# Prologue of a linear-attention and two-MoE kernel: the three chunks' TensorE work interleaved, five masks moved to ScalarE and GpSimd, products of ones added

## The chip, the cores and the metric

The kernel runs on one core of a Trainium2 chip. The metric is the device time of one execution in microseconds (us), as the median of several runs. The engines are called as in the profile: PE (TensorE, matmul; PEld is its weight load), DVE (VectorE), ACT (ScalarE), POOL (GpSimd) and SP (SyncE, which only issues transfers here).

## What is computed

Gated linear attention over 4 batches, 8 heads, 768 positions and a head size of 48; a dense two-layer network with squared ReLU on the 3072 tokens; then a layer of 8 experts of which each token takes one.

```python
def _attn_ref(q, k, v, f_logit):
    f = 1.0 / (1.0 + np.exp(-f_logit))
    for t in range(S):
        state = f[:, :, t, :, None] * state + np.einsum('bhd,bhe->bhde', k[:, :, t], v[:, :, t])
        y[:, :, t] = np.einsum('bhd,bhde->bhe', q[:, :, t], state)

x = attn_out.transpose(0, 2, 1, 3).reshape(B * S, H * D)    # 3072 x 384
h = np.maximum(x @ w_in, 0.0)                               # w_in 384 x 2048
x = h * h @ w_out                                           # w_out 2048 x 384
# experts: argmax of x @ w_gate, then relu(x @ w1[e]) @ w2[e], times the token's gate
```

## The kernel before, in words

The attention is worked in chunks of 128 tokens, 24 in all, and three chunks make a token group of 384 (`G`); there are 8 groups. A chunk has these steps, each a function of the kernel:

- `load_chunk(c)`: SP asks for f (the gate logits), q and k (one tile, `qk`, of three that take turns) and v.
- `sigmoid(c)` on ACT, then `decays(c)` on DVE: two scans of 112 x 517 with small operations between (lines 216 to 225), then `scale_qk(c)`, which multiplies k and q by the running products (lines 235 to 237).
- `scores(c)` on PE: k is transposed (`pk`, line 257), copied to `kt` by ACT (259), and k times q is made for all heads (`pa`, 264). `masked(c)` on DVE multiplies `pa` by the causal mask (271).
- `outputs(c)` on PE: the state times q (300), `pu` = k times v for the next state (310), the masked scores times v (320). In group 0 a product with `spread` (331) puts two of the heads' rows where the dense layer wants them; in other groups two transfers do that (336). ACT copies the result to `xT` (328 to 333).
- `state(c)` on DVE makes the next state `wst` from `pu` (345 to 348).

The dense layer goes over 16 hidden blocks i per group: `moe_h` makes `ph` (line 395 in group 0, plain float32, each product in two instructions; 405 in the others, split into high and low parts), `moe_act` squares it on ACT to `gg`, and `moe_out` makes `po` (435), two blocks behind `moe_h`. In group 0 the weights come in as 64-bit numbers: `stage_job(n)` asks for job n's stage `stg` (line 185, three stages at most), and `convert_job(n)` turns it into `w_raw` with three DVE operations (167, 170, 173) and asks for stage n + 3. Job 2j is a piece of w_in, job 2j + 1 one of w_out, and each serves the hidden blocks 2j and 2j + 1.

Order: PE, ACT, DVE and POOL take their instructions in the order in which the program writes them, SP's is set by a scheduler. The prologue (lines 567 to 601) does chunks 0, 1 and 2 with jobs 0 to 2. Then the loop over groups runs the dense layer of group g, with the attention of group g + 1 put between its blocks by `attention_group`, at fixed block numbers `b`:

```python
b = (1, 6, 10)[m] if g == 1 else 5 * m
while not (yield) == (b, 1):
    pass
```

At `(b, 1)`, after block b, come the scores and the mask of a chunk, at `(b + 1, 0)` the next chunk's decays, at `(b + 2, 1)` its outputs and state, and at `(b + 3, 0)` the next chunk's scaling. In group 0 each block also converts one job, from job 3 on.

Of the kernel before, what the change touches and what calls it, by code (L numbers as in the profile page):

```python
# [57 lines left out]
def gla_moe_moe_kernel(ctx: ExitStack, tc: tile.TileContext, qk, ft, vt, w_in, w_out, w_gate, w_gateT, w_e, q, k, v, f_logit, out, dbg=None):  # L58
# [11 lines left out]
    spread = const.tile([128, 3, 128], F32, name="spread")  # L70
    nc.gpsimd.memset(spread, 0.0)
    for r in range(3):
        for o in (0, 64):
            nc.gpsimd.tensor_copy(spread[:, r, o + D : o + 64], ident[:, o + r : o + D : 3])
# [12 lines left out]
    step_r = const.tile([PR, FL], BF16, name="step_r")
    nc.gpsimd.memset(step_r, PFLOOR)
    nc.gpsimd.memset(step_r[:, ::SEG], 1.0)
    step_f = const.tile([PR, FL], F32, name="step_f")  # L90
    nc.gpsimd.memset(step_f, PFLOOR)
# [55 lines left out]

    ld_t = {}

    def load_chunk(c):  # L150
        t = qk_t[c % 3]
        f = ld.tile([PR, FL], F32, tag="f", name="f")
        v3 = ld.tile([128, H, 64], F32, tag="v", name="v")
        nc.sync.dma_start(out=f, in_=ft[c])
        for i in ((1, 2), (0, 1)) if c == 0 else ((0, 2),):
            for j in range(2):
                nc.sync.dma_start(out=t[64 * j : 64 * j + D, slice(*i)], in_=qk[c, D * j : D * j + D, slice(*i)])
        nc.sync.dma_start(out=v3, in_=vt[c])
        ld_t[c] = t, f, v3

# [69 lines left out]
    def scale_qk(c):  # L230
        t, pr, _ = ld_t[c]
        tl, _ = prep_t[c]
        pairs = lambda a: a.rearrange("p (a b) -> p a b", a=4)
        qd, kd = t[:, 0], t[:, 1]
        nc.vector.tensor_tensor(out=kd, in0=kd, in1=pairs(tl[:, 1:FL])[:, :, 1:], op=ALU.mult)
        nc.vector.tensor_tensor(out=qd, in0=qd, in1=pairs(pr[:, 0 : FL - 1])[:, :, 1:], op=ALU.mult)
        nc.vector.tensor_tensor(out=pmin[0:PR], in0=pmin[0:PR], in1=tl[:, 1:FL:SEG], op=ALU.min)

    def x_tiles(g):
        xT = (  # L240
            xhp.tile([128, 3, G], F32, tag="xl", name="xT0")
            if g == 0
            else xp.tile([128, 3, G], F32, tag="xT", name="xT")
        )
        x_t[g] = xT, xp.tile([128, G], F32, tag="xT3", name="xT3")
# [1 line left out]

    at_t = {}

    def scores(c):  # L250
        t, _, _ = ld_t[c]
        qd, kd = t[:, 0], t[:, 1]
        kt = None
        if c % CPB != CPB - 1:
            pk = ps_a.tile([128, 4, PR], F32, tag="att", name="pk")
            for p in range(4):
                nc.tensor.transpose(out=pk[:, p, :], in_=kd[:, p, :], identity=ident[0:PR, 0:PR])  # L257
            kt = a1.tile([128, 4, PR], F32, tag="kt", name="kt")
            nc.scalar.activation(out=kt, in_=pk, func=AF.Copy)
        pas = [ps_a.tile([128, 4, 128], F32, tag="att", name="pa") for _ in range(2)]  # L260
# [16 lines left out]
    def outputs(c):
        g, m = divmod(c, GC)
        first = c % CPB == 0
        t, _, v3 = ld_t.pop(c)  # L280
        qd = t[:, 0]
        kt, at = at_t.pop(c)
# [8 lines left out]
        if g == 0:  # L291
            y[2] = ps_o.tile([128, DM], F32, tag=f"po{m}", name="y2")[:, 0:C]
        opens = (0, 2, 3) if g == 0 else (0, 2)
        closes = (3,) if g == 0 else (1, 3)
        if not first:
            for s in range(2):
                for b in range(2):
                    for j in range(2):
                        rows, p = slice(64 * j, 64 * j + D), 2 * s + b
                        nc.tensor.matmul(  # L300
                            y[2 * j + s][64 * b : 64 * b + 64],
                            lhsT=wst[c % 2][rows, p, :],
                            rhs=qd[rows, p, :],
                            start=2 * j + s in opens,
                            stop=False,
                        )
        if pu is not None:
            for p in range(4):
                for j in range(2):
                    nc.tensor.matmul(  # L310
                        pu[64 * j : min(64 * j + 64, PR), p, :],
                        lhsT=kt[:, p, 64 * j : min(64 * j + 64, PR)],
                        rhs=v3[:, p + 4 * j, 0:D],
                        start=True,
                        stop=True,
                    )
        for n in (2, 3, 0, 1):
            for b in range(2):
                j, p = n // 2, 2 * (n % 2) + b
                nc.tensor.matmul(  # L320
                    y[n][64 * b : 64 * b + 64],
                    lhsT=v3[:, p + 4 * j, :],
                    rhs=at[:, j, p, :],
                    start=first and n in opens,
                    stop=n in closes,
                )
# [12 lines left out]
    def state(c, pu):
        if pu is None:  # L340
# [242 lines left out]
    pu = outputs(0)  # L583
# [790 lines left out]
```

## Time and profile before

| what | value |
|---|---|
| median of 3 runs (lowest, highest) | 805.92 us (803.7, 806.31) |
| the profiled execution's own time | 804.5 us |
| span of the profiled execution | 802.8 us |
| PE busy | 775.1 us, 97% |
| DVE busy | 561.3 us, 70% |
| ACT busy | 413.4 us, 51% |
| POOL busy | 76.2 us, 9% |
| chain that ended last, shares by engine | PE 85%, issue 6%, DVE 4%, DMA 2% |

The span runs from the first to the last instruction; the rest of the execution's time lies around it. A line of the timeline gives start and duration in us, engine, line, operation, what it writes and reads, and how many instructions were merged; in brackets the engine's idle time before it and what ended that. Ends of PE's instructions are modelled, and POOL's times are rough.

### The profile page before, as it was taken

What the parts mean: (1) busy time and instruction counts of PE and PEld (TensorE: products, weight loads), DVE (VectorE), ACT (ScalarE), POOL (GpSimd) and SP (SyncE); (2) the same over time, 40 slices, a digit from 0 to 9 for tenths busy, and PEclk for the clock granted to TensorE, in tenths of its full rate; (3) what the DMA queues carried; (4) which work ended last, traced back from release to release, by engine and by line L of the source; (5) the groups of instructions that cost most, each with busy time, mean ns of one, the idle gap of its engine ahead of it and who ended that gap; (6) DMA issues with size and microseconds to landing.
All of it is one profiled execution on the core that took longest, in us unless ns stands there. A gap on an engine that the chain in (4) does not pass through costs nothing.

```text
span 802.8 us, 15135 instructions
## 1 busy us (share of the span) xinstructions
PE 775.1 (97%) x5657; PEld 723.2 (90%) x5657; DVE 561.3 (70%) x1309; ACT 413.4 (51%) x822; POOL 76.2 (9%) x108
## 2 busy tenths in 40 slices
PE   5899999999999999999999999999999999999994
PEld 4566579999999999999999999998999999999994
DVE  7999689768757767857757844668566676666650
ACT  2224376454464454455455454762566666666651
POOL 2000000000000000000000002000432232223110
PEclk9999999999999999999999999999999999999997
DMA  9787511111130121130120015321877777776760
GB/s 274 216 262 231 142 40 41 52 53 51 40 91 26 45 82 46 45 101 27 46 71 1 1 39 199 110 76 52 289 221 224 220 219 228 211 213 208 212 205 18
DMA packets 39410, 98.93 MB, mean 123 GB/s; under 512 B 5502, under 2 KB 9314, under 8 KB 39200
## 3 DMA queue, kind: packets, MB, share of 16 engines
q1 hardware_dynamic: 35744, 88.42, 37.3%
q0 software_dynamic: 3584, 9.46, 3.3%
q8 instruction: 46, 0.75, 0.4%
q14 instruction: 36, 0.29, 0.1%
HBM read 88.16 MB, written 10.24 MB: 123 GB/s over the span
## 4 chain that ended last, share of the span: by engine, by line
PE 85%; issue 6%; DVE 4%; DMA 2%; POOL 1%; ACT 1%; POOLq 0%; SPq 0%; DVEq 0%; ACTq 0%
PE po L435 25%; PE ph L405 23%; PE ph L982 11%; PE qo L1002 11%; PE ph L395 3%; PE pa L264 3%; PE py L320 3%; PE py L300 1%; PE pu L310 1%; DMA xT<-xT 1%; PE px L642 1%; PE pk L257 1%; DMA out<-o,ids 1%; PE pl L485 0%; DVE tl L216 0%
## 5 line engine op out<-in xcount | busy, mean ns | idle before, releaser
L411 ACT ACTIVATE gg<-ph 128x384 f32<-128x384 f32 x128 | 62.8, 491 | 184.6 <-PE ph L405 134.0
L614 DVE TENSOR_TENSOR w_lo<-raw,w_hi 128x768 fp32r<-128x768 f32 x112 | 107.0, 957 | 31.7 <-ACT w_hi L613 31.7
L418 DVE TENSOR_TENSOR gl<-gg,gh 128x384 fp32r<-128x384 f32 x112 | 62.1, 555 | 85.3 <-ACT gh L416 84.0
L405 PE MATMUL ph<-xh,w_lo 128*128 128x384 f32 x336 | 118.7, 353 | 0.9 <-ACT gg L411 0.9
L405 PE MATMUL ph<-xl,w_hi 128*128 128x384 f32 x336 | 114.4, 341 | 0.6 <-DVE xl L163 0.6
L405 PE MATMUL ph<-xh,w_hi 128*128 128x384 f32 x336 | 113.9, 339 | 0.0
L435 PE MATMUL po<-w_hi,gl 128*128 128x384 f32 x336 | 113.4, 338 | 0.0
L435 PE MATMUL po<-w_hi,gh 128*128 128x384 f32 x336 | 113.2, 337 | 0.0
L435 PE MATMUL po<-w_lo,gh 128*128 128x384 f32 x336 | 112.8, 336 | 0.0
L986 ACT ACTIVATE hh<-ph 128x256 fp32r<-128x256 f32 (+1 forms) x120 | 44.3, 370 | 103.3 <-PE ph L982 91.5
L613 ACT ACTIVATE w_hi<-raw 128x768 fp32r<-128x768 f32 x112 | 93.6, 837 | 0.0
L982 PE MATMUL ph<-xh,w_lo 128*128 128x256 f32 x312 | 88.9, 285 | 0.0
L982 PE MATMUL ph<-xl,w_hi 128*128 128x256 f32 x312 | 87.6, 281 | 0.0
L982 PE MATMUL ph<-xh,w_hi 128*128 128x256 f32 x312 | 87.5, 280 | 0.0
L459 DVE SCALAR_TENSOR_TENSOR junk<-rows,wgb 128x384 f32<-128x384 f32 x144 | 79.9, 555 | 3.3
L987 DVE SCALAR_TENSOR_TENSOR hl<-ph,hh 128x256 fp32r<-128x256 f32 (+1 forms) x120 | 48.7, 405 | 42.4 <-ACT hh L986 39.5
L1002 PE MATMUL qo<-w_hi,hl 128*128 128x384 f32 x208 | 70.4, 339 | 0.0
L1002 PE MATMUL qo<-w_hi,hh 128*128 128x384 f32 x208 | 70.4, 338 | 0.0
L1002 PE MATMUL qo<-w_lo,hh 128*128 128x384 f32 x208 | 70.1, 337 | 0.0
L412 ACT ACTIVATE gg<-gg 128x384 f32<-128x384 f32 x128 | 67.3, 526 | 4.1
L405 PEld LDWEIGHTS ph<-xh,w_lo 128*128 128x128 f32 x336 | 63.0, 188 | 6.9 <-issue 3.1
L405 PEld LDWEIGHTS ph<-xl,w_hi 128*128 128x128 f32 x336 | 63.1, 188 | 1.0 <-DVE xl L163 0.8
(235 smaller groups left out, 1498.0 us busy)
## 6 DMA issues: line engine op xcount, KB each, us to landing
raw<-w_e SPq DMA_DIRECT2D x120, 384.0 KB, 3.6
qk<-qk SPq DMA_DIRECT2D x46, 192.0 KB, 3.6
v<-vt SPq DMA_DIRECT2D x24, 256.0 KB, 3.7
stg<-w_in SPq DMA_DIRECT2D x8, 768.0 KB, 6.1
stg<-w_out SPq DMA_DIRECT2D x8, 768.0 KB, 6.0
f<-ft SPq DMA_DIRECT2D x24, 226.2 KB, 3.1
xs<-rows SPq DMA_DIRECT2D x8, 577.5 KB, 3.3
wgb<-w_gateT SPq DMA_DIRECT2D x1, 1536.0 KB, 7.1
```

The lines of the kernel that those rows point to most:

```text
L405: nc.tensor.matmul(ph, lhsT=w[:, sl], rhs=x[:, k, :], start=(n == 0), stop=(n == 8))
L411: nc.scalar.activation(out=gg, in_=ph, func=AF.Relu)
L412: nc.scalar.activation(out=gg, in_=gg, func=AF.Square)
L418: nc.vector.tensor_tensor(out=gl, in0=gg, in1=gh.bitcast(F32), op=ALU.subtract)
L435: nc.tensor.matmul(po[m], lhsT=a[:, sl], rhs=w[:, ws], start=(i == 0 and n == 0), stop=(i == NF - 1 and n == len(terms) - 1),)
L459: nc.vector.scalar_tensor_tensor(out=junk, in0=rows[:, m, 0:DM], scalar=1.0, in1=wgb[0][:, e, :], op0=ALU.mult, op1=ALU.mult, accum_out=lg ...
L613: nc.scalar.activation(out=hi, in_=src, func=AF.Copy)
L614: eng.tensor_tensor(out=lo, in0=src, in1=hi.bitcast(F32), op=ALU.subtract)
L982: nc.tensor.matmul(ph, lhsT=wslice(s, w, (i * 3 + k) * 128, 128), rhs=x[:, k, :], start=(n == 0), stop=(n == 8))
L986: nc.scalar.activation(out=hh, in_=ph, func=AF.Relu)
L987: nc.vector.scalar_tensor_tensor(out=hl, in0=ph, scalar=0.0, in1=hh.bitcast(F32), op0=ALU.max, op1=ALU.subtract)
L1002: nc.tensor.matmul(out_t[s][m], lhsT=x[:, sl], rhs=wslice(s, w, 3 * F2 + i * DM, DM), start=(i == 0 and n == 0), stop=(i == 7 and n == 2),)
```

## The change

Five things, all but the last two in the prologue.

- POOL sets `step_r` and `step_f` first; `spread` is filled after chunk 0's mask.
- The three chunks' steps are cut into smaller functions and interleaved on PE. The chunks' outputs of group 0 go to the three banks that the dense layer's `po` uses, `pu` of chunks 0 and 1 to the banks of `ph`. f of chunk 1 is asked for ahead of v of chunk 0.
- 72 and then 24 products of a tile of ones with itself (bfloat16, 128 x 128) are issued on PE, before chunk 0's transposes and before chunk 1's. Nothing reads them.
- The masks of chunks 0, 1, 3, 4 and 5 are made in two steps: ACT copies the scores to SBUF, and POOL's `affine_select` sets the upper part to 0.
- Jobs 0, 1 and 2 are converted after chunk 2's outputs, and chunk 3's decays, state and scaling leave the prologue: they now come at blocks 0 and 1 of the loop, and chunk 3's scores at block 2 (before: block 1).

```diff
+    step_r = const.tile([PR, FL], BF16, name="step_r")
+    nc.gpsimd.memset(step_r, PFLOOR)
+    nc.gpsimd.memset(step_r[:, ::SEG], 1.0)
...
     def masked(c):
         kt, pas = at_t[c]
         at = a1.tile([128, 2, 4, 128], F32, tag="at", name="at")
         for j in range(2):
-            nc.vector.tensor_tensor(
-                out=at[:, j], in0=pas[j], in1=mask[:, None, :].to_broadcast([128, 4, 128]), op=ALU.mult
-            )
+            if c in (0, 1, 3, 4, 5):
+                nc.scalar.activation(out=at[:, j], in_=pas[j], func=AF.Copy)
+                nc.gpsimd.affine_select(
...
+                )
+            else:
...
+    def first_banks(c):
+        po = [ps_o.tile([128, DM], F32, tag=f"po{m}", name="y") for m in range(GC)]
+        first_y[c] = [po[0][:, 0:C], po[0][:, C : 2 * C], po[2][:, 0:C], po[1][:, 0:C]]
+
+    def first_key_values(c):
+        if c < GC - 1:
+            pu = ps_h.tile([128, G], F32, tag="ph", name="pu")[:, 0 : 4 * D]
+        else:
+            pu = ps_a.tile([128, 4 * D], F32, tag="att", name="pu")
...
+    def first_values(c):
+        y, ts = first_y[c], slice(c * C, (c + 1) * C)
+        scores_values(c, y, (3, 2, 0, 1), () if c else (0, 2, 3), (3,))
+        nc.scalar.activation(out=x_t[0][1][:, ts], in_=y[3], func=AF.Copy)
+
+    def first_rows(c):
+        xT, xT3 = x_t[0]
+        y, ts = first_y[c], slice(c * C, (c + 1) * C)
+        for r in range(3):
+            nc.tensor.matmul(y[r], lhsT=spread[:, r, :], rhs=xT3[:, ts], start=False, stop=r > 0)
+        for r in (2, 0, 1):
+            nc.scalar.activation(out=xT[:, r, ts], in_=y[r], func=AF.Copy)
...
     def attention_group(g):
         for m in range(GC):
             c = g * GC + m
-            b = (1, 6, 10)[m] if g == 1 else 5 * m
+            b = (2, 6, 10)[m] if g == 1 else 5 * m
+            if c == GC:
+                while not (yield) == (0, 1):
+                    pass
+                decays(c)
+                while not (yield) == (1, 1):
+                    pass
+                state(c - 1, first_pu.pop(c - 1))
+                scale_qk(c)
...
+    def fill(n):
+        for _ in range(n):
+            nc.tensor.matmul(idle[:, 0:128], lhsT=ones_bf, rhs=ones_bf, start=True, stop=True)
+
+    fill(72)
     x_tiles(0)
     sigmoid(0)
     sigmoid(1)
     decays(0)
     scale_qk(0)
+    key_rows(0)
     scores(0)
-    sigmoid(2)
     decays(1)
     masked(0)
...
+    first_key_values(0)
+    fill(24)
+    sigmoid(2)
     scale_qk(1)
-    state(0, pu)
+    state(0, first_pu[0])
+    key_rows(1)
+    first_banks(0)
+    first_values(0)
     scores(1)
     decays(2)
     masked(1)
-    pu = outputs(1)
+    first_rows(0)
+    first_key_values(1)
     scale_qk(2)
-    state(1, pu)
+    state(1, first_pu[1])
+    key_rows(2)
+    first_banks(1)
+    state_queries(1, first_y[1], (0, 2, 3))
     scores(2)
+    first_values(1)
+    masked(2)
+    first_rows(1)
+    first_key_values(2)
+    first_banks(2)
+    state_queries(2, first_y[2], (0, 2, 3))
+    first_values(2)
+    first_rows(2)
     load_chunk(3)
     convert_job(0)
-    masked(2)
-    pu = outputs(2)
-    sigmoid(3)
     load_chunk(4)
     convert_job(1)
-    decays(3)
-    state(2, pu)
-    scale_qk(3)
     convert_job(2)
+    sigmoid(3)
```

How the order moves is told at three places. On SP, before, from chunk 3's f on. qk0, qk1, qk2 are the tiles of chunks 3, 4 and 5 here, stg_346 is the stage of job 3, stg_396 that of job 4:

```order
L154 DMA f_336<-ft 112x517
L157 DMA qk0_148<-qk 48x1024 x2
L154 DMA f_386<-ft 112x517
L158 DMA v_337<-vt 128x512
L157 DMA qk1_149<-qk 48x1024 x2
L154 DMA f_443<-ft 112x517
L158 DMA v_387<-vt 128x512
L185 DMA stg_346<-w_out 128x768
L157 DMA qk2_150<-qk 48x1024 x2
L185 DMA stg_396<-w_in 128x3x256
L158 DMA v_444<-vt 128x512
```

The same place of the changed program, where stg_487 is job 3's stage and stg_499 job 4's:

```order
L149 DMA f_477<-ft 112x517
L160 DMA qk0_142<-qk 48x1024 x2
L149 DMA f_489<-ft 112x517
L163 DMA v_479<-vt 128x512
L149 DMA f_566<-ft 112x517
L160 DMA qk1_143<-qk 48x1024 x2
L163 DMA v_491<-vt 128x512
L160 DMA qk2_144<-qk 48x1024 x2
L163 DMA v_568<-vt 128x512
L190 DMA stg_487<-w_out 128x768
L190 DMA stg_499<-w_in 128x3x256
```

The stage of job 3 stood ahead of q, k and v of chunk 5, and now stands behind them.

On DVE, before, from job 1 (the first three rows) to the scaling of chunk 3's k and q; the mask of chunk 2 and job 0 stand ahead of these rows:

```order
L167 TENSOR_SCALAR w_raw<-stg 128x768
L170 SCALAR_TENSOR_TENSOR w_raw<-stg,w_raw 128x768
L173 SCALAR_TENSOR_TENSOR w_raw<-stg,w_raw 128x768
L216 SCALAR_TENSOR_TENSOR tl<-f,step_r 112x517
L220 RECIPROCAL step_f<-tl 112x4
L224 COPY em<-tl 112x4
L225 SCALAR_TENSOR_TENSOR f<-f,step_f 112x517
L347 TENSOR_TENSOR wst_106<-pu,wst_105 112x4x48
L348 TENSOR_TENSOR wst_106<-wst_106,em 112x4x48
L235 TENSOR_TENSOR qk_148<-qk_148,tl 112x512
L236 TENSOR_TENSOR qk_148<-qk_148,f 112x512
```

The changed program, from the last row of job 3 on; jobs 0, 1 and 2 stand ahead of job 3, and ahead of them the mask of chunk 2:

```order
L178 SCALAR_TENSOR_TENSOR w_raw<-stg,w_raw 128x768
L221 SCALAR_TENSOR_TENSOR tl<-f,step_r 112x517
L225 RECIPROCAL step_f<-tl 112x4
L229 COPY em<-tl 112x4
L230 SCALAR_TENSOR_TENSOR f<-f,step_f 112x517
L172 TENSOR_SCALAR w_raw<-stg 128x768
L175 SCALAR_TENSOR_TENSOR w_raw<-stg,w_raw 128x768
L178 SCALAR_TENSOR_TENSOR w_raw<-stg,w_raw 128x768
L401 TENSOR_TENSOR wst_100<-pu,wst_99 112x4x48
L402 TENSOR_TENSOR wst_100<-wst_100,em 112x4x48
L240 TENSOR_TENSOR qk_142<-qk_142,tl 112x512
L241 TENSOR_TENSOR qk_142<-qk_142,f 112x512
```

Between the mask of chunk 2 and the scaling of chunk 3 stood one job (job 0 came ahead of the mask); now five do, jobs 0 to 4.

On PE, before, from the first two blocks' ph on (x6 is two blocks):

```order
L395 MATMUL ph<-xT_186,w_raw 128x384 x6
L257 MATMUL pk<-ident,qk_148 128x112 x4
L264 MATMUL pa<-qk_148 128x128 x8
L395 MATMUL ph<-xT_186,w_raw 128x384 x3
L435 MATMUL po_489<-w_raw,gg 128x384
L435 MATMUL po_490<-w_raw,gg 128x384
L435 MATMUL po_491<-w_raw,gg 128x384
L395 MATMUL ph<-xT_186,w_raw 128x384 x3
```

The changed program, from the first three blocks' ph on:

```order
L458 MATMUL ph<-xT_253,w_raw 128x384 x9
L498 MATMUL po_558<-w_raw,gg 128x384
L498 MATMUL po_559<-w_raw,gg 128x384
L498 MATMUL po_560<-w_raw,gg 128x384
L261 MATMUL pk<-ident,qk_142 128x112 x4
L273 MATMUL pa<-qk_142 128x128 x8
L458 MATMUL ph<-xT_253,w_raw 128x384 x3
```

Chunk 3's transposes and scores moved from ahead of the third ph to behind the first po, directly ahead of the fourth ph.

## Rows read from the trace of the kernel before

**Rows 1.** Timeline, first 30 us: the sigmoid on ACT, then DVE's scan and masks.
```profile
4.10 0.64 ACT L210 ACTIVATE f<-f 112x517 f32<-112x517 f32 x1 [2.00 <-DMA f<-ft]
...
5.85 1.24 DVE L216 TENSOR_TENSOR_SCAN tl<-f,step_r 112x517 f32<-112x517 f32 x1 [1.46 <-POOL step_r L89]
...
20.06 1.29 DVE L271 TENSOR_TENSOR at<-pa,mask 128x512 f32<-128x512 f32 x2 [2.06 <-PE pa L264]
...
25.66 1.28 DVE L271 TENSOR_TENSOR at<-pa,mask 128x512 f32<-128x512 f32 x2
```

**Rows 2.** Timeline, 18 to 42 us: PE.
```profile
18.11 1.91 PE L264 MATMUL pa<-qk 48*128 48x128 f32 x16
...
30.07 4.14 PE L395 MATMUL ph<-xT,w_raw 128*128 128x384 f32 x12 [0.64 <-ACT xT L333]
...
34.64 0.58 PE L257 MATMUL pk<-ident,qk 112*128 112x112 f32 x4 [0.43 <-PE ph L395]
...
35.29 1.16 PE L264 MATMUL pa<-qk 48*128 48x128 f32 x16
...
37.82 2.17 PE L395 MATMUL ph<-xT,w_raw 128*128 128x384 f32 x6 [1.37 <-DVE w_raw L173]
...
41.77 2.10 PE L395 MATMUL ph<-xT,w_raw 128*128 128x384 f32 x6
```

**Rows 3.** Stretches: start:end and length, engines' busy time, PEclk, DMA share, GB/s.
```profile
0.00:10.00 10.00, 0.75 (x4) 0.66 (x4) 6.88 (x11) 2.55 (x3) 5.38 (x30) 1.00 0.79 203
...
20.00:30.00 10.00, 8.74 (x130) 6.91 (x128) 9.16 (x15) 2.07 (x8) 0.00 (x0) 1.00 0.95 260
```

**Rows 4.** Timeline, SP's issues: stages of jobs 1 and 2, v of chunk 4.
```profile
8.82 0.35 SPq L185 DMA_DIRECT2D stg<-w_out  x1
...
9.65 0.56 SPq L185 DMA_DIRECT2D stg<-w_in  x1
...
23.00 1.47 SPq L158 DMA_DIRECT2D v<-vt  x1
```

**Rows 5.** Transfers by size and us to landing: of rows 4, all stages, all loads.
```profile
stg<-w_out SPq DMA_DIRECT2D x1, 768.0 KB, 8.5
...
stg<-w_in SPq DMA_DIRECT2D x1, 768.0 KB, 9.9
...
v<-vt SPq DMA_DIRECT2D x1, 256.0 KB, 4.5
...
DMA to landing us min/median/max: 4.4/6.1/9.9
...
qk<-qk SPq DMA_DIRECT2D x46, 192.0 KB, 3.6
...
f<-ft SPq DMA_DIRECT2D x24, 226.2 KB, 3.1
```

**Rows 6.** Timeline, 30 to 38 us: DVE from chunk 3's decays to job 3.
```profile
30.58 1.24 DVE L216 TENSOR_TENSOR_SCAN tl<-f,step_r 112x517 f32<-112x517 f32 x1 [1.18 <-ACT f L210]
...
33.21 0.33 DVE L347 TENSOR_TENSOR wst<-pu,wst 112x192 f32<-112x192 f32 x1
...
33.86 0.69 DVE L235 TENSOR_TENSOR qk<-qk,tl 112x512 f32<-112x512 f32 x1
...
35.14 0.55 DVE L167 TENSOR_SCALAR w_raw<-stg 128x768 uint32<-128x768 uint32 x1
...
37.59 0.55 DVE L167 TENSOR_SCALAR w_raw<-stg 128x768 uint32<-128x768 uint32 x1
```

**Rows 7.** Timeline, 102 us: PE's first product of token group 1.
```profile
102.46 0.45 PE L405 MATMUL ph<-xh,w_lo 128*128 128x384 f32 x1 [0.88 <-ACT gg L411]
```

**Rows 8.** Stretches after PE's last product.
```profile
794.00:796.00 2.00, 0.00 (x0) 0.00 (x0) 0.00 (x0) 0.00 (x0) 0.00 (x0) 0.64 0.21 61
796.00:798.00 2.00, 0.00 (x0) 0.00 (x0) 0.00 (x0) 0.00 (x0) 0.00 (x0) 0.50 0.00 0
```

**Rows 9.** Timeline, 4 us: the select that makes the causal mask on POOL.
```profile
3.88 0.28 POOL L77 TENSOR_SCALAR_AFFINE_SELECT mask<-mask 128x128 bf16<-128x128 bf16 x1
```

More of the change, by code (lines that the diff above doesn't have):

```diff
@@ L64, in gla_moe_moe_kernel @@
     xs = dram.tile([NT, ROW], F32, name="xs")
+    step_r = const.tile([PR, FL], BF16, name="step_r")
+    nc.gpsimd.memset(step_r, PFLOOR)
+    nc.gpsimd.memset(step_r[:, ::SEG], 1.0)
+    step_f = const.tile([PR, FL], F32, name="step_f")
+    nc.gpsimd.memset(step_f, PFLOOR)
     ident = const.tile([128, 128], F32, name="ident")
     make_identity(nc, ident)
[L70 to L74, printed above, removed]
     mask = const.tile([128, 128], BF16, name="mask")
@@ L86, in gla_moe_moe_kernel @@
     nc.vector.memset(ones_bf, 1.0)
[L87 to L91, printed above, removed]
+    spread = const.tile([128, 3, 128], F32, name="spread")
+    nc.gpsimd.memset(spread, 0.0)
     rev = const.tile([128, GC, NE], F32, name="rev")
@@ L259, in scores @@
             nc.scalar.activation(out=kt, in_=pk, func=AF.Copy)
+        at_t[c] = kt, None
+    def scores(c):
+        t, _, _ = ld_t[c]
+        qd, kd = t[:, 0], t[:, 1]
         pas = [ps_a.tile([128, 4, 128], F32, tag="att", name="pa") for _ in range(2)]
@@ L270, in masked, with key_values, state_queries, scores_values @@
         for j in range(2):
-            nc.vector.tensor_tensor(
-                out=at[:, j], in0=pas[j], in1=mask[:, None, :].to_broadcast([128, 4, 128]), op=ALU.mult
-            )
-        at_t[c] = kt, at
+            if c in (0, 1, 3, 4, 5):
+                nc.scalar.activation(out=at[:, j], in_=pas[j], func=AF.Copy)
+                nc.gpsimd.affine_select(
+                    out=at[:, j],
+                    in_=at[:, j],
+                    pattern=[[0, 4], [1, 128]],
+                    compare_op=ALU.is_ge,
+                    fill=0.0,
+                    base=0,
+                    channel_multiplier=-1,
+                )
+            else:
+                nc.vector.tensor_tensor(
+                    out=at[:, j], in0=pas[j], in1=mask[:, None, :].to_broadcast([128, 4, 128]), op=ALU.mult
+                )
+        at_t[c] = kt, at
+    def key_values(c, pu):
+        kt, _ = at_t[c]
+        v3 = ld_t[c][2]
+        for p in range(4):
+            for j in range(2):
+                nc.tensor.matmul(
+                    pu[64 * j : min(64 * j + 64, PR), p, :],
+                    lhsT=kt[:, p, 64 * j : min(64 * j + 64, PR)],
+                    rhs=v3[:, p + 4 * j, 0:D],
+                    start=True,
+                    stop=True,
+                )
+    def state_queries(c, y, opens):
+        qd = ld_t[c][0][:, 0]
+        for s in range(2):
+            for b in range(2):
+                for j in range(2):
+                    rows, p = slice(64 * j, 64 * j + D), 2 * s + b
+                    nc.tensor.matmul(
+                        y[2 * j + s][64 * b : 64 * b + 64],
+                        lhsT=wst[c % 2][rows, p, :],
+                        rhs=qd[rows, p, :],
+                        start=2 * j + s in opens,
+                        stop=False,
+                    )
+    def scores_values(c, y, order, opens, closes):
+        _, _, v3 = ld_t.pop(c)
+        _, at = at_t.pop(c)
+        for n in order:
+            for b in range(2):
+                j, p = n // 2, 2 * (n % 2) + b
+                nc.tensor.matmul(
+                    y[n][64 * b : 64 * b + 64],
+                    lhsT=v3[:, p + 4 * j, :],
+                    rhs=at[:, j, p, :],
+                    start=n in opens,
+                    stop=n in closes,
+                )
     def outputs(c):
@@ L290, in outputs @@
         y = [py[0][:, 0, :], py[0][:, 1, :], py[1][:, 0, :], py[1][:, 1, :]]
[L291 to L294, printed above, removed]
         if not first:
[L296 to L306, printed above, removed]
-        if pu is not None:
[L308 to L326, printed above, removed]
+            state_queries(c, y, (0, 2))
+        if pu is not None:
+            key_values(c, pu)
+        scores_values(c, y, (2, 3, 0, 1), (0, 2) if first else (), (1, 3))
         ts = slice(m * C, (m + 1) * C)
         nc.scalar.activation(out=xT3[:, ts], in_=y[3], func=AF.Copy)
-        if g == 0:
-            for r in range(3):
-                nc.tensor.matmul(y[r], lhsT=spread[:, r, :], rhs=xT3[:, ts], start=False, stop=r > 0)
         nc.scalar.activation(out=xT[:, 2, ts], in_=y[2], func=AF.Copy)
         nc.scalar.activation(out=xT[:, 0:2, ts], in_=py[0], func=AF.Copy)
-        if m == GC - 1 and g:
+        if m == GC - 1:
             for o in (0, 64):
@@ L573, in gla_moe_moe_kernel @@
     nc.sync.dma_start(out=wg, in_=w_gate)
+    idle = ps_h.tile([128, G], F32, tag="ph", name="idle")
+    def fill(n):
+        for _ in range(n):
+            nc.tensor.matmul(idle[:, 0:128], lhsT=ones_bf, rhs=ones_bf, start=True, stop=True)
+    fill(72)
     x_tiles(0)
@@ L578, in gla_moe_moe_kernel @@
     scale_qk(0)
+    key_rows(0)
     scores(0)
-    sigmoid(2)
     decays(1)
     masked(0)
-    pu = outputs(0)
+    for r in range(3):
+        for o in (0, 64):
+            nc.gpsimd.tensor_copy(spread[:, r, o + D : o + 64], ident[:, o + r : o + D : 3])
+    first_key_values(0)
+    fill(24)
+    sigmoid(2)
     scale_qk(1)
-    state(0, pu)
+    state(0, first_pu[0])
+    key_rows(1)
+    first_banks(0)
+    first_values(0)
     scores(1)
```

24 lines of the change are left out of this document (15 added, 9 removed).

## The prediction

> **What bounds the kernel now.** I read the engines' busy shares first, then the stretches, then the first 45 us instruction by instruction, DVE and PE beside each other, and last the transfers. From 41.77 us on PE runs without a gap worth naming to the end of token group 0; there it waits 0.88 us [rows 7], and past that this change touches nothing. So a change to the prologue is worth what it moves the moment from which PE is never again short of work. Before, that moment is the product ph of the third hidden block at 37.82, which had waited 1.37 us for weights that DVE still had to convert [rows 2]. The reader is to see three things in the first 40 us. PE is late: in the first 10 us it works 0.75, and its first ph starts at 30.07 [rows 2, 3]. DVE is busy 9.16 of 10 us in the stretch from 20 to 30, and the DMA engines 0.95 [rows 3]. And a stage of weights (stg) needs 4.4 to 9.9 us from its request to its landing, the 9.9 for the one asked for at 9.65 [rows 4, 5]: the transfers queue behind each other.
>
> I compare one landmark, because the order of PE's work is the same from there but for one shift of chunk 3's outputs: the **fourth ph** (i=3), which starts at 41.77 before [rows 2].
>
> **The change, step by step.**
>
> DVE's start. Its first scan began at 5.85, after 1.46 us idle for GpSimd's step_r; the sigmoid that it also needs ended at 4.10 + 0.64 = 4.74 [rows 1]. With step_r set first, the scan starts at 4.8: 1.05 us earlier.
>
> DVE up to the first conversion. The mask of chunk 2 stood at 25.66. Ahead of it go: 1.05; the masks of chunks 0 and 1, 2 x 1.29; the wait of 2.06 for pa [rows 1]; and job 0, which moves behind the mask, 2.45 (35.14 to 37.59 [rows 6]). That is 25.66 - 8.14 = 17.5. Now pa of chunk 2 is late next: q is scaled about 1 us before, and PE has 8 state products and pa (1.16 [rows 2]) to do, so I put the mask at 18.7 and job 0 at 20.0. Jobs 0, 1 and 2 end at 20.0 + 3 x 2.45 = 27.35.
>
> PE up to its fourth product. Before, 4.4 us lay between chunk 2's mask and the first ph (25.66 to 30.07). So it starts at 23.1, or up to 1.4 later because chunk 2's state products now wait for chunk 1's rows to leave the dense banks. Two ph take 4.14 [rows 2], the third waits for job 2 and takes half of that, and po(0), of the same 6 rows, as long. By about 32 PE has done what stood done at 41.77 before, but for pk and pa of chunk 3, which take 1.8. That would be a gain of some 8 us.
>
> **Where it stops.** PE's next instruction is pk of chunk 3, and it needs k scaled by DVE. Before, only two jobs stood ahead of that on DVE; now five do, jobs 0 to 4, with the decays between jobs 3 and 4. PE takes its work in order, so the fourth ph stands behind this pk though its weights are ready. And job 3 needs the stage w_out(1), whose request moved on SP: before it stood ahead of q, k and v of chunk 5, now behind all loads of chunks 3, 4 and 5. The request itself waits for PE to release v of chunk 2, at about 23.5, not later than job 0 allows. When it lands:
> - The third stage landed at 9.65 + 9.9 = 19.55, v of chunk 4 at 23.00 + 4.5 = 27.5 [rows 4, 5]. Between them 3 f, 4 qk halves and 2 v landed, 678.6 + 768 + 512 = 1958.6 KB [rows 5] in 7.95 us: 246 KB/us.
> - Chunk 5's qk and v now come before the stage: 640 KB, 2.6 us, so 30.1. A stage behind a stage took 19.55 - (8.82 + 8.5) = 2.2: 32.3. The requests of chunks 3 to 5 are now made sooner, so I take 32.0. Lower end: 23.5 + 4.4 = 27.9, the quickest stage of before; upper 23.5 + 9.9 = 33.4, the slowest.
>
> From there DVE runs: job 3 2.45, decays 2.63 (30.58 to 33.21), job 4 2.45, state 0.65, so k of chunk 3 starts at 40.2; pk started 0.78 after k did, and pa ended 1.81 after pk's start (34.64 to 36.45) [rows 2, 6]. The fourth ph starts at **42.8**, 1.0 us later than before. PE has then stood idle for about 9 us where it had 1.37.
>
> The clock after that gap. At the end of the run, with PE idle, the granted clock reads 0.64 and then 0.50, which is 1.2 GHz [rows 8]; while PE works it reads 1.00, 2.4 GHz [rows 3]. PE's 9 us of idleness here are of that kind, so I expect a restart at 1.2 GHz. What it costs no row shows: below nothing, if the clock were back at once; above, the start of the run: pa took 1.91 us at 18.11 and 1.16 at 35.29 [rows 2], so PE, at work since 9.25 (its 0.75 us of the first 10 [rows 3]), was slow to 20 us, and half of these 10.8 us is 5.4. (The granted clock's column reads 1.00 there too; I go by the rows' durations.) After 42 PE's work is dense, where at the start it was short and broken by waits; I take 4 us at half speed, a cost of 2.0.
>
> The end of group 0. DVE loses three masks there, 3 x 1.29 us, which is no gain while PE is the bound; but its last conversion comes sooner, and the loads that the transition waits for with it. Of the 0.88 us I take 0.7 back; ends 0 and 0.88.
>
> Edits at nothing. A GpSimd select of 128 columns takes 0.28 [rows 9], one of 512 between that and 1.12. Chunk 3's two, behind two ScalarE copies of at most a mask's 0.65, have ph, po, ph, po (4 x 1.94) as cover. The four of chunks 0 and 1 (at most 4.5) lie in the slack between 27.35 and 32.0. So do the products of ones: 72 at no more than a slow pa row's 1.91 / 16 = 0.12 end by 9.7 where pk wants to start at 8.2 (9.25 less 1.05), and the 24 take at most 2.9; if all of that came together it would use the slack up, and 1 to 5 us would be added. v of chunk 0, moved behind f of chunk 1, lands before its product. Kept warm or not, a faster prologue PE ends in the same wait for the stage.
>
> **Sum**: 1.0 + 2.0 - 0.7 = +2.3 us. The profiled execution took 804.5 us, 1.7 of it outside its span, so 806.8 against its own time. It lies 1.4 us under the median of 805.92; the runs after will scatter like those, so I name **808.2 us**. A difference under 0.3% (2.4 us) can't be told from none here, and my forecast stands on that edge.
>
> **Rivals.**
> - *Faster: the stage is not late.* If the loads stream faster than 246 KB/us, job 3 never waits: stage at 27.3, fourth ph 10.8 us later at 38.1, a gain of 3.7, less 0 to 2 of clock as the gap is still 4 us: 802.2 to 804.2. For it: two stages did land 2.2 us apart, 350 KB/us. Against: it is chunk loads that stand ahead, and these went at 246. It decides from a landing before 29 us on. The Trainium skill (SBUF — State Buffer, "The DMA setup-cost knee") has a rule that would bring this about: a transfer takes some 2 us and its bytes at 436 GB/s; as an estimate by it chunk 5's 640 KB would take 1.5 us and not 2.6, and the queue would be empty when the stage is asked for. The trace bears that out for no chunk load.
> - *Clearly slower: the clock stays low as long as at the start.* 1.0 + 5.4 - 0.7 = +5.7, 811.6. For it: pa's slow rows to 20 us. Against: PE's work there was broken. It decides from 5 us at 1.2 GHz on.
> - *No clock cost* (and the change then does what it says, only into a wait): 1.0 - 0.7, +0.3, 806.2. Against: the drop [rows 8].
>
> **How the numbers follow.** The likeliest, stalled with 1 to 3.5 us of clock: 0.50, split 0.22 same and 0.28 slower by the edge of 2.4 us. Clock as at the start: 0.15, slower. No clock cost: 0.15, same. Stage not late: 0.20, of which 0.15 faster and 0.05 same. So faster 0.15, same 0.42, slower 0.43. The range, 803.4 to 811.4, leaves out half of the fast case and a little of the slow one; the likeliest case alone is 807 to 810.
>
> **What would show it.** DVE's first scan at 4.8; job 0 at 20 and not 23.2; the first ph at 23 to 24.5; then on DVE an idle time before job 3 that ended with the stage's landing near 32; on PE an idle time of 7 to 10 us before chunk 3's pk, and the fourth ph near 42.8; the granted clock below 1.00 in that gap, and ph rows of more than 2.1 us after it. The prediction is wrong if the stage lands by 29, if pk of chunk 3 starts before 38, or if the clock costs over 4 us.

## The result, and the profile after

The changed kernel takes **810.56 us** (median of 5, 809.8 to 812.93) against 804.53 for the kernel before, timed beside it (5 runs, 803.7 to 806.31): ratio 1.0068, 95% interval 1.0051 to 1.0086, some 6 us slower. The profiled execution is the longest of the five: 812.93, span 811.1 (before: 802.8).

In the changed kernel a job's three DVE operations are lines 172, 175 and 178, the scans 221 and 230, the scaling of k and q 240 and 241, pk 261, pa 273, the prologue's outputs 334 and 389, ph 458 and po 498. In the experiments' kernels these numbers differ by some lines.

PE's timeline of the change from the first ph to po(1) (columns as in the rows of before: start, duration, engine, line, what is written and read, count, and in brackets the idle time ahead of it), then po(1) of the kernel before:

```profile
25.61 6.43 PE L458 MATMUL ph<-xT,w_raw 128*128 128x384 f32 x18 [0.54 <-ACT xT L391]
31.88 2.10 PE L498 MATMUL po<-w_raw,gg 128*128 128x384 f32 x6
46.01 1.01 PE L261 MATMUL pk<-ident,qk 112*128 112x112 f32 x4 [12.03 <-DVE qk L240]
46.95 2.08 PE L273 MATMUL pa<-qk 48*128 48x128 f32 x16
48.95 3.83 PE L458 MATMUL ph<-xT,w_raw 128*128 128x384 f32 x6
52.62 2.10 PE L498 MATMUL po<-w_raw,gg 128*128 128x384 f32 x6
```
```profile
43.70 2.10 PE L435 MATMUL po<-w_raw,gg 128*128 128x384 f32 x6
```

The first ph starts 4.5 us earlier than before (30.07 [rows 2]), and PE is through three ph and po(0) at 33.98. Then it stands still for 12.03 us, until DVE has scaled k of chunk 3. The fourth ph comes at 48.95 (41.77 before [rows 2]) and po(1) at 52.62, 8.9 us later than the 43.70 of before. pk, pa and ph take 1.01, 2.08 and 3.83 us where they took 0.58, 1.16 and 2.10.

DVE's timeline of the change (the same columns), from chunk 2's mask to the scaling of chunk 3:

```profile
21.07 1.29 DVE L293 TENSOR_TENSOR at<-pa,mask 128x512 f32<-128x512 f32 x2 [1.73 <-PE y L334]
...
28.76 0.96 DVE L178 SCALAR_TENSOR_TENSOR w_raw<-stg,w_raw 128x768 uint32<-128x768 uint32 x1
37.07 0.56 DVE L172 TENSOR_SCALAR w_raw<-stg 128x768 uint32<-128x768 uint32 x1 [7.35 <-DMA stg<-w_out]
...
39.54 1.23 DVE L221 TENSOR_TENSOR_SCAN tl<-f,step_r 112x517 f32<-112x517 f32 x1
...
42.17 0.54 DVE L172 TENSOR_SCALAR w_raw<-stg 128x768 uint32<-128x768 uint32 x1
...
45.27 0.68 DVE L240 TENSOR_TENSOR qk<-qk,tl 112x512 f32<-112x512 f32 x1
```

Before, DVE scanned chunk 3 at 30.58, scaled it at 33.86 and only then took job 3, at 37.59 [rows 6]. Now it ends job 2 at 29.7, waits 7.35 us for job 3's stage, and runs job 3, the decays, job 4, the state and the scaling one after the other.

Why the stage is late: some of the requests on SP, then what SP waited for in the stretches 23 to 24.8 and 29 to 30, then the landing times (KB, us from request to landing) of the transfers asked for at 10.83, 18.27 and 29.09:

```profile
10.83 0.56 SPq L190 DMA_DIRECT2D stg<-w_in  x1
18.27 0.35 SPq L163 DMA_DIRECT2D v<-vt  x1
23.85 0.78 SPq L160 DMA_DIRECT2D qk<-qk  x2
29.09 0.35 SPq L190 DMA_DIRECT2D stg<-w_out  x1
```
```profile
SPq L160 <- DMA stg<-w_in: 3.3, 1, 3.3
SPq L190 <- DMA v<-vt: 1.2, 1, 1.2
```
```profile
stg<-w_in SPq DMA_DIRECT2D x1, 768.0 KB, 13.0
v<-vt SPq DMA_DIRECT2D x1, 256.0 KB, 10.8
stg<-w_out SPq DMA_DIRECT2D x1, 768.0 KB, 8.0
```

Job 0 set a stage buffer free at 24.8, but the stage of job 3 was asked for only at 29.09, when the v asked for at 18.27 had landed (18.27 + 10.8 = 29.07). In the same way qk of chunk 4 left at 23.85, when the stage asked for at 10.83 had landed (10.83 + 13.0 = 23.83). Between the two of each pair stand seven other transfers (a chunk's qk is two): in this trace SP has eight in flight and asks for the ninth when the first of them is there. When eight take 7 to 13 us to land, every request behind them is held up, whatever engine has released its buffer. The stage then took 8.0 us and landed at 37.1.

The stretches of the gap and behind it (length, busy time and count of PE, PEld, DVE, ACT, POOL, then granted clock, DMA share, GB/s):

```profile
36.00:38.00 2.00, 0.00 (x0) 0.00 (x0) 0.89 (x2) 0.00 (x0) 0.00 (x0) 1.00 1.08 417
38.00:40.00 2.00, 0.00 (x0) 0.00 (x0) 1.97 (x3) 0.00 (x0) 0.00 (x0) 0.66 0.50 204
50.00:52.00 2.00, 2.00 (x4) 1.09 (x4) 1.26 (x1) 0.71 (x2) 0.99 (x2) 0.50 0.71 183
52.00:54.00 2.00, 2.00 (x7) 1.05 (x7) 1.97 (x5) 1.02 (x2) 0.00 (x0) 0.93 0.55 212
```

PE is idle from 33.98 to 46.01. The granted clock reads 1.00 up to 38, 0.66 in the next stretch and then 0.50, which is 1.2 GHz, also while PE works again, until 0.93 in the stretch from 52 on. It is the fall that the end of the run of before shows [rows 8].

### The profile page after: what moved, and what is told of

The parts are those of the page before. It is cut to its first block, busy times and chain, and to the rows that moved or that the text cites. A ratio compares the mean times of both kernels' runs of the same rounds, so it can differ in the third digit from the quotient of the medians.

```text
span 811.1 us, 15348 instructions
## 1 busy us (share of the span) xinstructions
PE 780.3 (96%) x5753; PEld 727.5 (90%) x5753; DVE 556.8 (69%) x1299; ACT 418.7 (52%) x835; POOL 87.2 (11%) x118
## 4 chain that ended last, share of the span: by engine, by line
PE 87%; issue 4%; DMA 4%; DVE 3%; ACT 1%; POOL 0%; POOLq 0%; SPq 0%; DVEq 0%; ACTq 0%
PE po L498 24%; PE ph L468 23%; PE ph L1068 12%; PE qo L1088 12%; PE pa L273 3%; PE ph L458 3%; PE py L334 2%; DMA v<-vt 1%; PE py L320 1%; PE pu L304 1%; PE pk L261 1%; DMA stg<-w_out 1%; DMA xT<-xT 1%; PE px L728 1%; PE idle L642 1%
```

## The experiments

Theory A is the prediction's: DVE and PE take their work in order, chunk 3's scaling stands behind two jobs of which the first waits for a stage, and the clock falls in the gap. All ratios are to the kernel before, timed beside each run, with 95% intervals.

**1. Chunk 3's decays first.**

```diff
-                decays(c)
...
-                state(c - 1, first_pu.pop(c - 1))
-                scale_qk(c)
...
+    sigmoid(3)
     convert_job(2)
-    sigmoid(3)
+    decays(3)
+    state(2, first_pu.pop(2))
+    scale_qk(3)
```

> Edit: decays, state and scaling of chunk 3 stand on DVE ahead of job 3 again, right behind job 2, as before the change; all else is the change's. Theory A (the loss is one chain: stage of job 3 lands at 37.0, DVE takes job 3 first, chunk 3's scaling and so pk and the fourth ph stand behind it): DVE runs the decays at 29.6 to 32.3 and scales k by about 33; pk of chunk 3 follows po(0) at about 34 with no gap, the fourth ph starts at about 36 (48.95 in the change), po(1) needs only job 1; the next wait is the fifth ph's for job 4, which ends at about 42, so the fifth ph starts near 42 instead of 54.56. The granted clock reads 1.00 throughout. Time 797 to 801 us. Rival B (the selects on GpSimd slow DVE's work on chunks 1 and 2, and the whole prologue is late for that): nothing of that is touched, so at most the clock's 3 us come back: 806 to 809. Rival C (transfers alone set the time: stages land too late in any order): the fifth ph waits for a stage that has moved with it, 808 to 811.

Measured: **799.63 us**, 0.9925 (0.9901 to 0.9949): 6 us faster than before and some 11.5 us (1.0068 less 0.9925) faster than the change. PE's timeline of this run:

```profile
32.12 2.10 PE L490 MATMUL po<-w_raw,gg 128*128 128x384 f32 x6
34.06 0.55 PE L261 MATMUL pk<-ident,qk 112*128 112x112 f32 x4
34.54 1.16 PE L273 MATMUL pa<-qk 48*128 48x128 f32 x16
35.63 2.20 PE L450 MATMUL ph<-xT,w_raw 128*128 128x384 f32 x6
37.67 2.10 PE L490 MATMUL po<-w_raw,gg 128*128 128x384 f32 x6
40.54 2.17 PE L450 MATMUL ph<-xT,w_raw 128*128 128x384 f32 x6 [0.78 <-DVE w_raw L178]
```

pk follows po(0) with no gap, the clock stays at 1.00, and 0.78 us for job 4 is all that is left of 12.03. The fourth ph starts at 35.63 (36 said), the fifth at 40.54 (42 said). Theory A holds; B and C fall. Job 3's stage was no help: asked for at 27.55, it landed 7.1 us later, at 34.65, as DVE came to it, inside the 34.20 to 36.20 of the runs that kept the change's order. It was late only for what stood behind it: job 3 itself serves po(2).

**2. The stage first.** Same change, with the loads of chunks 4 and 5 behind job 3's stage on SP (`behind` orders each of those loads of f, qk and v after that request, without a wait):

```diff
-        nc.sync.dma_start(out=v3, in_=vt[c])
+        behind(nc.sync.dma_start(out=v3, in_=vt[c]), c)
...
```

> Edit: on SP the loads of chunks 4 and 5 stand behind the request of job 3's stage; all else is the change's (DVE still takes job 3 ahead of the decays of chunk 3). Theory A: the request goes out at about 24.8, when job 0 is done, instead of 29.09, and about 1 MB less stands ahead of it, so it lands at 29 to 31 instead of 37.0. DVE's wait of 7.35 us before job 3 shrinks to about 1; but the stages of jobs 4 and 5 now stand behind the loads of chunks 4 and 5, job 4 starts at 36 to 38 and chunk 3's scaling behind it, pk at 40 to 42 instead of 46.0. Time 803 to 807. Rival B (selects): unchanged, 809 to 812. Rival C (transfers alone, total bytes set the time): the same bytes stand ahead of the last stage that is waited for, 809 to 812.

Measured: 808.93, 1.0035 (1.0018 to 1.0053), above A's 803 to 807 and just below the 809 of the rivals. The stage was asked for at 24.82 and DVE began job 3 at 29.63 without a wait. But job 4's stage was now late, and PE restarted into the low clock:

```profile
38.11 0.56 DVE L186 TENSOR_SCALAR w_raw<-stg 128x768 uint32<-128x768 uint32 x1 [3.30 <-DMA stg<-w_in]
```
```profile
41.97 1.01 PE L277 MATMUL pk<-ident,qk 112*128 112x112 f32 x4 [8.00 <-DVE qk L256]
42.91 2.08 PE L289 MATMUL pa<-qk 48*128 48x128 f32 x16
44.92 4.21 PE L474 MATMUL ph<-xT,w_raw 128*128 128x384 f32 x6
```

Curing the late transfer alone gets back 2.7 us of 11.5 by the ratios (1.0068 less 1.0035): the next late stage takes its place, which is the part of C that holds, and behind a gap of 8.00 us the rows are again those of half the clock.

**3, 4. Products of ones in the gap**, first 160, then 215 (`warm` multiplies the tile of ones with itself into a bank of the attention's):

```diff
+            if c == GC:
+                warm(160)
             key_rows(c)
```

> Edit: 160 further products of ones on TensorE between po(0) and pk of chunk 3, in the gap of 12.03 us; all else is the change's. At 0.063 us each (24 took 1.51) they run from 34.0 to about 44. Theory A: the gap's end does not move (pk at 46.0), but the granted clock stays at 1.00, so pk, pa and the fourth ph take 0.58, 1.16 and 2.10 instead of 1.01, 2.08 and 3.83: the clock's part of the loss, 3.1 us, comes back, 807 to 808. Rival D (the clock costs more than its rows show, or less): 804 if it is the whole loss, 810.5 if nothing.

Measured with 160: 810.45, 1.0055 (1.0037 to 1.0074): the gap's clock loss was not won back. Its PE timeline and stretches:

```profile
33.78 9.10 PE L649 MATMUL warm<-ones_bf 128*128 128x128 bf16 x160
45.13 0.60 PE L261 MATMUL pk<-ident,qk 112*128 112x112 f32 x4 [2.26 <-DVE qk L240]
45.73 1.31 PE L273 MATMUL pa<-qk 48*128 48x128 f32 x16
46.98 3.70 PE L460 MATMUL ph<-xT,w_raw 128*128 128x384 f32 x6
```
```profile
43.00:46.00 3.00, 0.87 (x8) 0.66 (x10) 2.97 (x7) 0.23 (x1) 0.00 (x0) 1.00 0.42 89
46.00:48.00 2.00, 2.00 (x18) 1.48 (x17) 1.93 (x3) 1.20 (x3) 0.22 (x1) 0.65 0.96 368
48.00:50.00 2.00, 2.00 (x4) 1.09 (x4) 1.45 (x2) 0.73 (x2) 1.29 (x2) 0.50 0.28 46
```

The products ended at 42.9, PE was idle for 2.26 us, and the clock fell **after** that gap, in a stretch in which PE was busy throughout (46 to 48): ph took 3.70. So this run does not price the clock.

> Edit: the change with 215 products of ones between po(0) and pk of chunk 3, instead of 160 in the earlier run, so that they fill the whole gap (12.0 us at 0.056 each, which the 160 showed). In that run TensorE was idle for 2.26 us behind the products and the clock fell after it all the same, so its price stayed open. Theory A (idle TensorE lowers the clock; price 3.1 us by the rows pk 1.01, pa 2.08, ph 3.83): the granted clock stays at 1.00, the rows are 0.58, 1.16, 2.10, and the time is 3 us under the change's: 807 to 808.5. Rival D (such products don't hold the clock, or it costs nothing in the end): 810 to 811.

Measured with 215: 810.09, 1.0053 (1.0033 to 1.0072). Now the clock stayed at 1.00 and the rows are those of full speed:

```profile
33.81 12.17 PE L649 MATMUL warm<-ones_bf 128*128 128x128 bf16 x215
45.81 0.56 PE L261 MATMUL pk<-ident,qk 112*128 112x112 f32 x4
46.30 1.16 PE L273 MATMUL pa<-qk 48*128 48x128 f32 x16
47.39 2.20 PE L460 MATMUL ph<-xT,w_raw 128*128 128x384 f32 x6
49.43 0.81 PE L500 MATMUL po<-w_raw,gg 128*128 128x384 f32 x2
```

From pk to po(1) it is 3.62 us here and 6.61 in the change (46.01 to 52.62): the **clock costs 3.0 us**. The two profiled executions bear it out: pk starts at nearly the same time (45.81 and 46.01), and the spans are 808.5 and 811.1, 2.6 apart. The median hardly fell, because the stage came sooner in this run (DVE scaled k at 42.40) and the products, fixed in number, held pk up until 45.81. I expected 807 to 808.5; the row behind A is borne out, its time is not. Filling a gap of unknown length gives back what it saves.

**5. The order alone, in the kernel before.**

```diff
-    decays(3)
-    state(2, pu)
-    scale_qk(3)
+    late_pu = [pu]
...
+                decays(c)
...
+                state(c - 1, late_pu.pop())
+                scale_qk(c)
```

> Edit, to the kernel before: chunk 3's decays, state and scaling behind jobs 3 and 4, and its scores one step later, as the change has them; nothing else of the change. On SP job 3's stage keeps its place ahead of chunk 5's loads. Theory A (the order on DVE and TensorE costs only what the stage is late): job 2 ends at 31.8, the stage landed at 30.4, so DVE doesn't wait; k of chunk 3 is scaled at about 40.0, pk follows at 40.8 behind a gap of 3 us, the fourth ph at 42.6 (41.77 before) and the outputs of chunk 3 come later: 805 to 808, within 1 us of before. Rival G (the order alone makes the change's loss): 809 to 812.

Measured: 809.82, 1.0048 (1.0031 to 1.0064): rival G, and not A as I had worked it out. In this run:

```profile
32.23 0.56 DVE L167 TENSOR_SCALAR w_raw<-stg 128x768 uint32<-128x768 uint32 x1 [1.58 <-DMA stg<-w_out]
```
```profile
41.21 0.98 PE L257 MATMUL pk<-ident,qk 112*128 112x112 f32 x4 [4.33 <-issue]
42.12 2.08 PE L264 MATMUL pa<-qk 48*128 48x128 f32 x16
44.13 3.90 PE L403 MATMUL ph<-xT,w_raw 128*128 128x384 f32 x6
47.86 2.10 PE L443 MATMUL po<-w_raw,gg 128*128 128x384 f32 x6
```

pk came at 41.21, near what I had worked out (40.8), though DVE did wait for the stage, 1.58 us; what I left out is the clock, which read 0.50 from 42 to 46 behind these 4.33 us of idle PE. po(1) starts 4.2 us later than before, about 3 of them the clock's. So where chunk 3's steps stand costs 0.0048 of the change's 0.0068 even with the rest of the prologue untouched.

**6. Scores later.** The change with `b = (3, 6, 10)`: pk, pa and chunk 3's outputs one block later on PE.

> Edit: the change with chunk 3's pk, pa and outputs one step later on TensorE, behind the fourth ph and po(1); DVE and SP keep the change's order. Theory A (TensorE is held only because it takes its work in order): the fourth ph and po(1) run at 34 to 38, since their weights are ready; the gap begins at 38 and ends where it did, with pk at 45 to 46; what was done by 54.5 is then done by 49 to 50, and the clock falls all the same: 805.5 to 808. Rival C (the transfers hold back everything): 810 to 812.

Measured: 807.33, 1.0015 (1.0000 to 1.0030).

```profile
44.91 1.01 PE L261 MATMUL pk<-ident,qk 112*128 112x112 f32 x4 [7.05 <-DVE qk L240]
```

The fourth ph ran at 33.82 and po(1) at 35.76; pk came at 44.91 after a gap of 7.05 us, and the next ph and po at 47.86 and 50.86 (54.56 and 56.49 in the change). PE's order was holding back work that was ready, as A has it, and the clock's cost remained: pk took 1.01 us, and the next ph 3.17.

**7. Without the products of ones.**

> Edit: the 72 and the 24 products of ones of the change are left out; all else is the change's. Theory A: the prologue's TensorE work runs at the rows of before again (pk 0.98, pa 2.08 and 1.91), chunk 2's products and job 0 come 1 to 2 us later, but DVE waits for the stage of job 3 anyway; that stage stands behind loads that wait for TensorE to release v, so it lands 0 to 2 us later: 810 to 813. Rival E (the products pay): slower by 3 to 5 us, 814 to 816. Rival F (the products only stand in the way): 807 to 809.

Measured: 809.46, 1.0049 (1.0032 to 1.0065). The first ph started at 26.81 instead of 25.61, but DVE waited 3.47 us for the stage all the same: the products are worth nothing while the stall is there. It came out 0.5 us below the range I gave, between A and F, and its interval overlaps the change's.

**8. The masks on DVE** (`if False:` for the chunks of the change).

> Edit: the change with the masks of chunks 0, 1, 3, 4 and 5 on DVE again (no ScalarE copy, no GpSimd select); all else is the change's. Theory A (one chain from job 3's stage): k and q of chunks 1 and 2 are scaled in 0.66 to 0.69 us each instead of 1.05 and 1.11, which gives back 1.6 us, and two masks of 1.29 stand on DVE's way to job 0: it starts about 1 us later than 22.27, and DVE's wait for the stage hides that; pk of chunk 3 stays at 45 to 47; 809 to 812 us. Rival B (GpSimd's selects are what makes the change slow): 804 to 807.

Measured: 812.15, 1.0082 (1.0063 to 1.0102), just above A's range; B falls. k and q of chunks 1 and 2 were scaled in 0.68 us each, the first ph came at 28.51, 2.9 us later than in the change, and the stall hid that too: pk at 44.77. Not all of these 2.9 us are the masks': the granted clock read 0.77 and 0.50 from 20 to 24 us, and the outputs' rows took 1.97 and 1.55 us where the change has 1.10 and 0.93.

**9 to 12. With the decays first, what are the other parts worth?** Four runs on top of run 1: the stage first as well; the masks of chunks 3 to 5 on DVE; no products of ones; and, with the stage first, chunk 2's mask off DVE too.

> Edit: both: chunk 3's decays, state and scaling ahead of job 3 on DVE, and the loads of chunks 4 and 5 behind job 3's stage on SP. In the run with the decays first (799.63) DVE went from chunk 3's scaling to job 3 at 34.65 without a wait, so theory A gives the earlier stage nothing more: the next limit is DVE's own sequence up to job 4, and job 4's stage, which lands near 38 when it stands behind the loads: 799 to 801. Rival C (transfers set the time): 796 to 798.

Measured (9): 801.07, 0.9946 (0.9929 to 0.9964), just above A's range: the stage's place is worth nothing once nobody waits for it.

> Edit: the run with the decays first, and the masks of chunks 3, 4 and 5 on DVE (those of 0 and 1 stay on ScalarE and GpSimd). With the selects of chunk 3, job 4's three instructions took 0.99, 1.26 and 0.96 us beside GpSimd instead of 0.55, 0.96 and 0.96, and the fifth ph waited 0.78 us for them. Theory A: that comes back, the fifth ph at about 39.8 instead of 40.54, and three masks of 1.29 go where DVE has time: 798.5 to 800 against 799.63. Rival: DVE's three masks come due at the end of group 0, where TensorE's idle time for gg was 0.53 us with them away and 0.88 before: 800 to 800.5.

Measured (10): 802.74, 0.9969 (0.9955 to 0.9982), slower than both expectations. Where group 0 ends and group 1 begins PE waited 2.24 us for gg (0.53 in run 1). What PE waited for goes back to DVE: its last conversion ended 0.9 us later than in run 1 (86.4 us for 85.5), the load of 1536 KB that waits for that and the two transfers to `xT` behind it were asked for later (`xT` at 88.48 for 86.92), and ACT, which makes the gg, stood waiting for them. Behind this wait the granted clock read 0.50 from 100 to 102 us and PE's rows took 0.52 us instead of 0.34: the first ph of group 1 came 1.9 us later than in run 1 (98.99 for 97.08), the first po behind it 3.1 (102.72 for 99.62). Job 3's stage came 1.30 us late in the profiled run, so the fifth ph was no earlier (40.73) and DVE was 0.9 us behind run 1 from there on; the mask of chunk 5 then filled the 1.65 us in which DVE stood idle in run 1. How much of the wait is the late stage's and how much the masks' this run does not separate; by the times the masks on ScalarE and GpSimd pay.

> Edit: the run with the decays first, without the 96 products of ones. With the stall gone the prologue is on the path: without the products pk and pa of chunks 0 and 1 run at half the clock, and the first ph starts 1 us later (26.81 against 25.58 in the pair of runs that had the stall). Theory A: 800.3 to 801.3, some 1 us above 799.63. Rival F (the products give nothing): 799 to 800. Rival E (they give several us): 802 or more.

Measured (11): 803.0, 0.9965 (0.9949 to 0.998): 3 us over run 1 by the ratios, so rival E's by the median, though the two intervals just meet. Its profiled execution, the shortest of its twelve (800.17), has the first ph at 27.29 instead of 25.86. So the products pay 1.4 us by the trace and more by the times; what the rest is I can't say.

> Edit: decays first, stage first, and the mask of chunk 2 on ScalarE and GpSimd too. Job 0 no longer stands behind that mask (1.73 us of waiting and 1.29 of work): it can start near 19.5, jobs 0 to 2 end near 27 to 28, chunk 3 is scaled 2 us sooner, and job 4 no longer holds up the fifth ph (0.62 to 0.78 us in the runs with the decays first). Theory A: 798 to 800. Rival (the select of chunk 2 slows job 0 beside it, 0.99 for 0.55 and 1.26 for 0.96, and its two steps are longer than the one on DVE, so the first ph is later): 800 to 802.

Measured (12): **798.67 us**, 0.9903 (0.9885 to 0.9920), the lowest median of all, 7 us under before; its interval lies below run 9's and overlaps run 1's. The first ph is 0.9 us later than in run 1 (26.76; GpSimd's select ended an idle time of 0.74), but chunk 3 is scaled at 30.71 and the fifth ph starts at 40.15 with no wait.

## Why the prediction came out as it did

The direction and the mechanism were right: a prologue that is ready sooner and then waits for job 3's stage, with pk of chunk 3 stuck behind it. The time, 808.2, was 2.4 us short. 810.56 lies outside the 807 to 810 of the likeliest case, and inside the whole range only because its upper end was set for a clock cost of 5.4 that did not come: that much is luck.

- *DVE's start*: first scan at 4.56 (4.8 said).
- *DVE up to job 0*: 22.27, not 20.0. I expected chunk 2's mask to wait for pa; it waited for a y product of chunk 1 instead (1.73 us, line 334), because `at` has one buffer and that product, now behind pa of chunk 2 on PE, reads it. And k and q of chunks 1 and 2 took 1.05 to 1.11 us each beside GpSimd's selects, where I had left them at before's duration (0.69 for k of chunk 3 [rows 6]).
- *PE's first part*: first ph at 25.61, not 23.1 to 24.5; through po(0) at 33.98, not 32.
- ***The step that failed***: "The request itself waits for PE to release v of chunk 2, at about 23.5". It left at 29.09. I looked at who frees the buffer and not at SP's eight transfers in flight. From the request on the landing took 8.0, about what I had put (23.5 to 32.0), so the whole 5 us of the stage come from that one term; k of chunk 3 was scaled at 45.27 instead of 40.2.
- *The spread*: in the other runs with the change's order on SP, job 3 started at 34.20 to 36.20 (34.39 without the products), so the profiled 37.07 is a late one, as its 812.93 us are.
- *The clock*: 3.0 us instead of 2.0, inside the ends I gave; 1.4 of it falls ahead of the fourth ph (2.94 from pk to ph in the change, 1.58 in run 4).
- *The end of group 0*: idle time for gg 0.64 instead of 0.88 [rows 7]: 0.24 regained, not 0.7.
- *The sum with what was measured*: the fourth ph 7.2 us later, of which 1.4 are the clock's, so 5.8 where I had 1.0; 3.0 where I had 2.0; 0.24 back where I had 0.7. That makes 8.6, against 8.4 between the two profiled executions (812.93 and 804.5); the medians lie 6.0 apart.
- *The slack*: I covered the selects and the products of ones with the wait for the stage. Runs 7 and 8 bear that out; without the wait (runs 10 and 11) the masks' place and the products both show in the time.

Of the rivals, *not late* fell: in stretches of 2 us from 20 to 32 us the loads moved at 185 to 262 GB/s with the DMA engines busy all the time, and the stage was asked for at 29.09. The Trainium skill's curve (SBUF — State Buffer, "The DMA setup-cost knee") is not borne out in this full queue: as an estimate by it a v of 256 KB takes 2.6 us, and the one above took 10.8. *No clock cost* fell with the rows of 1.01, 2.08 and 3.83. *Clearly slower* came nearest, 811.6, for the wrong reason: the clock cost 3, not 5.4, and the stage the rest.

What I named but did not weigh is that the change moved chunk 3's decays behind jobs 3 and 4 though PE's next work, pk, pa, the fourth ph and po(1), needs neither job. With the decays back, the rest of the change is 6 us faster than the kernel before.

## What to carry to other kernels

When an edit makes one engine ready sooner, read for the next in-order engine what stands ahead of the operand it will ask for first, and put work that waits for a transfer behind work that doesn't. Count the transfers in flight ahead of a request, not only the buffer that it needs. Before dropping a part of a change that lost time, undo the one step that made the new wait: here the same change less one move went from 0.7% slower to 0.75% faster.

## What the runs showed of the hardware

GpSimd's and VectorE's instructions slow each other here. DVE's and POOL's timelines of the change, during chunk 0's selects, and last POOL's selects of chunk 3:

```profile
11.28 1.05 DVE L240 TENSOR_TENSOR qk<-qk,tl 112x512 f32<-112x512 f32 x1
12.26 1.11 DVE L241 TENSOR_TENSOR qk<-qk,f 112x512 f32<-112x512 f32 x1
```
```profile
10.38 2.45 POOL L283 TENSOR_SCALAR_AFFINE_SELECT at<-at 128x512 f32<-128x512 f32 x2 [4.24 <-ACT at L282]
12.79 2.31 POOL L656 COPY spread<-ident 128x16 f32<-128x16 f32 x6
49.77 1.22 POOL L283 TENSOR_SCALAR_AFFINE_SELECT at<-at 128x512 f32<-128x512 f32 x2 [31.71 <-ACT at L282]
```

The scaling, with two inputs in SBUF, takes 0.67 to 0.69 us when POOL is idle and 1.05 to 1.11 beside it; a pair of selects takes 1.22 us at 49.77, where DVE is idle for most of it, and 2.45 here; six copies to `spread` 2.31 (0.90 in the kernel before). In run 1 a job's first two operations took 0.99 and 1.26 beside a select instead of 0.55 and 0.96. The Trainium skill (SBUF — State Buffer, "Who interferes with whom") says so: a VectorE instruction with two SBUF inputs contends with a GpSimd instruction that reads SBUF. The trace agrees, with both sides longer; the job's first operation, a `tensor_scalar`, has one input, and the page counts its kind among those that can take the shared pair of ports.

The granted clock fell in run 3 while PE was busy again, behind a gap of 2.26 us; behind gaps of 12.03, 8.00 and 4.33 us (the change, runs 2 and 5) it read 0.50 or 0.69 at the restart, and in run 1, with a gap of 0.78 us, 1.00 throughout. It takes no long gap: in run 10 it fell behind idle times of 2.24 and 0.58 us close together, and in run 8 in a stretch of full work (20 to 22 us) behind one in which PE was idle for half of 2 us, while behind the 1.37 us of the kernel before [rows 2] it stayed at 1.00. The length of the gap just ahead does not settle it. Products of a 128 x 128 tile of ones ran at 0.080 us each at the start (72 in 5.77) and at 0.057 later (160 in 9.10).
